# One Strassen level more in two places of a fused attention and MLP kernel, accumulator banks seeded by copies, and an instruction order that was searched

## The chip, the core and the metric

The kernel runs on one core of a Trainium2 chip. The metric is the device time of one execution in microseconds (us). A run gives several executions and I quote their median. An execution is marked slow when it is over 1.5% above the fastest of the same kernel. All other executions are marked fast; ratios use fast ones alone. The kernel before is run again beside every experiment on the same chip, and its median moved between 302.9 and 304.5 us, with single executions between 300.3 and 307.3. So differences under about 1% need the ratio to the kernel before with its interval.

The profile counts the work of four engines side by side: TensorE (PE; its weight loads are PEld), VectorE (DVE), ScalarE (ACT) and GpSimd (POOL), before the change busy for 94, 78, 59 and 34% of the span. The rows of a fifth, SyncE (SP), are here issues of transfers only.

## The reference, cut to what matters

```python
# q, k, v: (8 batches, 8 heads, 576 rows, 64); w_in: (512, 2048); w_out: (2048, 512)
def phi(x, c, s):                       # "features": 64 -> 128 columns
    r = np.maximum(x, 0.0)
    return np.concatenate([r * c, r * s], axis=-1)
kv  = einsum(phi(k), v);  z = sum(phi(k))
num = einsum(phi(q), kv); den = einsum(phi(q), z) + 1e-06
x = (num / den)                         # rearranged to (4608 tokens, 512)
h = x @ w_in                            # layer 1
g = h * np.cos(h)                       # "gate"
out = g @ w_out                         # layer 2, (4608, 512) fp32
```

A batch gives four tiles of 128 tokens and a rest of 64. The kernel forms nine groups of 512 tokens: 0 to 7, one per batch, and "r", which gathers the rests. The order of the groups is 0, 1, 2, 3, 4, 5, 6, r, 7.

## The kernel before

Every piece of work is an operation with a duration in us, an engine (or a choice of engines), what it depends on and which buffers it takes. A list scheduler walks through time and always gives the engine that is free first the ready operation of the best priority. The sequence that comes out is written, in that order, as the program of each engine.

```python
def run(self, cold=0.0):                        # class Plan, cut
    while ready:
        cand = []
        for o in ready:
            t = max([o.at] + [d.end + d.lat for d in o.deps])
            ...                                 # buffers free?
            for e, us in o.alts.items():
                cand.append((max(t, clock.get(e, 0.0)), e, us, o, t))
        t0, e0 = min((c[0], c[1]) for c in cand)
        t, _, us, o, _ = min((c for c in cand if c[1] == e0 and c[0] <= t0 + self.EPS),
                             key=lambda c: (..., c[3].prio, c[0]))
        ...
```

Layer 1 is plain: for each of 16 blocks of 128 rows of h, four matmuls of 512 columns, a sine on ACT (the cosine), a product on DVE (the gate).

```python
def moe1(key, g, js, cs, s0, s1):               # layer 1, TensorE
    for n, j in enumerate(js):
        for c in cs:
            nc.tensor.matmul(ps[key][:, n, :], lhsT=w_in_sb[:, c, j * P:(j + 1) * P],
                             rhs=x[:, c, s0:s1], start=(c == 0 and n == 0), ...)
def gate(key, dst):
    nc.vector.tensor_tensor(out=dst, in0=ps[key], in1=cosine, op=ALU.mult)
```

Layer 2 of groups 1 to 7 and r is one Strassen level: seven products of half the size instead of eight. It needs sums of the gates (1024 elements per partition each, SBUF to SBUF, all on DVE) and sums of finished products (five per group on DVE). Layer 2 of group 0 is plain.

```python
def sums(g, c, n):                              # sums of gates, always DVE
    out, in0, in1, op = ((s1, a21, a22, ALU.add), (s2, s1, a11, ALU.subtract),
                         (a21, a11, a21, ALU.subtract), (a12, a12, s2, ALU.subtract))[n]
    nc.vector.tensor_tensor(out=out, in0=in0, in1=in1, op=op)
...
e6 = op({"V": 0.69}, EV, lambda e: add(part(g, "u2"), g, "Y", "s1"), ...)   # 1 of 5 adds
```

## Time and profile before

| | before |
|---|---|
| device time, median (range) | 304.47 us (304.13 to 307.12) |
| span of the profiled execution | 298.7 us |
| matmuls; their issue time | 2565; 269.5 us |
| gaps on TensorE | 23.0 us, of it 1.2 at half clock |
| first matmul; last matmul to the end | 1.0 us; 5.0 us |

**Issue and gaps.** In the trace the starts of back-to-back matmuls lie 216 ns apart at 512 columns, 109 at 256, 56 at 128, about 30 at 65. The number of matmuls of each width times these is the issue time. What a distance between two starts has more than that is a gap. Where the gap falls in a stretch for which the trace records the half clock I count it, up to one interval per matmul, as half clock; the rest is a wait. I computed these sums from the matmul records.

The page's first two parts, before: busy us and share of the span, then the busy tenths of each engine in 40 slices of the span, and the TensorE clock in tenths.

```profile
PE 280.1 (94%) x2565; PEld 201.3 (67%) x2565; DVE 233.7 (78%) x450; ACT 175.6 (59%) x303; POOL 102.0 (34%) x107
...
PE   8879999899969987999979999999999999999993
...
DVE  1878888899995798887869798987786786768661
...
POOL 1370004396191686287077194011002001100500
PEclk9979999999999999999999999999999999999998
```

TensorE is the bottleneck. From 157 us on its row is all nines but for the last slice: after 200 us the gaps add up to 0.2 us.

What TensorE waited for, before (us in total, times, longest us):

```profile
engine line waited for: us in total, times, longest us
PE N L228 <- DVE x L241: 2.8, 2, 2.1
PE M L279 <- ACT xT L159: 2.6, 1, 2.6
PE PY L337 <- DVE s L309: 2.2, 2, 1.6
```

These are a numerator behind a ratio on DVE, layer 1 behind transposed x, and layer 2 behind a sum of gates.

The DVE sums of gates, before, by source line (count: shortest/median/longest ns, first and last start in us):

```profile
L309 DVE TENSOR_TENSOR s<-g x14: 680/681/1116, 71.6 to 283.0; 128x1024 f16<-128x1024 f16 x14
L309 DVE TENSOR_TENSOR s<-s,g x14: 679/681/1008, 73.4 to 283.8; 128x1024 f16<-128x1024 f16 x14
L309 DVE TENSOR_TENSOR g<-g x14: 676/682/684, 75.2 to 284.4; 128x1024 f16<-128x1024 f16 x14
L309 DVE TENSOR_TENSOR g<-g,s x14: 680/682/976, 81.3 to 287.8; 128x1024 f16<-128x1024 f16 x14
```

A sum takes 0.68 us. The longest reach 1.1 us, beside work on POOL.

Two stretches, before (start:end, length, then busy us of each engine, clock, DMA share, GB/s):

```profile
30.00:65.00 35.00, 33.68 (x330) 24.06 (x328) 30.32 (x69) 24.70 (x44) 11.68 (x16) 1.00 0.95 276
200.00:299.00 99.00, 93.94 (x679) 65.05 (x676) 67.52 (x105) 34.84 (x59) 10.45 (x20) 0.99 0.18 61
```

### The profile page before, as it was taken

To read this page: it belongs to the slowest core of one execution; us is meant where nothing else is said; L and a number is where in the kernel's file an instruction comes from. 1 tells how busy PE (TensorE), PEld (TensorE's weight loads), DVE (VectorE), ACT (ScalarE), POOL (GpSimd) and SP (SyncE) were. 2 spreads that over 40 slices of the span, in tenths; PEclk is the share of its full clock that TensorE was granted. 3 is DMA by queue.
4 is the path that set the end of the run, shared out by engine and by line. 5 is a ranking of instruction groups with operands and counts; after the bars stand their busy time and mean duration, and the time that the engine had idled before them with its cause. 6 is when DMAs were issued, how large, how long until landed. Compare 5 with 4: busy or idle time off the path is not lost.

```text
span 298.7 us, 6583 instructions
## 1 busy us (share of the span) xinstructions
PE 280.1 (94%) x2565; PEld 201.3 (67%) x2565; DVE 233.7 (78%) x450; ACT 175.6 (59%) x303; POOL 102.0 (34%) x107
## 2 busy tenths in 40 slices
PE   8879999899969987999979999999999999999993
PEld 8768856688855555566646666776666666566782
DVE  1878888899995798887869798987786786768661
ACT  2846748599379797679489497634433443443210
POOL 1370004396191686287077194011002001100500
PEclk9979999999999999999999999999999999999998
DMA  7799995897899999999999999715202100200213
GB/s 218 264 163 203 204 362 183 279 308 120 273 274 235 356 232 169 283 278 203 322 256 202 238 369 195 141 47 151 35 0 94 48 1 32 111 2 0 91 52 140
DMA packets 77086, 53.29 MB, mean 178 GB/s; under 512 B 46080, under 2 KB 74752, under 8 KB 77056
## 3 DMA queue, kind: packets, MB, share of 16 engines
q1 hardware_dynamic: 69760, 39.73, 55.2%
q0 software_dynamic: 6848, 12.59, 16.6%
q10 hardware_dynamic: 448, 0.57, 0.5%
q8 instruction: 20, 0.33, 0.5%
q14 instruction: 10, 0.08, 0.1%
HBM read 36.74 MB, written 9.44 MB: 155 GB/s over the span
## 4 chain that ended last, share of the span: by engine, by line
PE 55%; DMA 16%; DVE 10%; POOL 5%; SPq 5%; ACT 4%; issue 3%; ACTq 0%; DVEq 0%
PE M L279 26%; DMA vm<-in_v_dram 13%; PE PY L337 8%; PE PZ L337 6%; PE PX L337 5%; PE M L376 5%; POOL qp L181 4%; DMA qm<-in_q_dram 3%; PE KV L219 2%; DVE g L292 2%; SPq L171 2%; DVE x L241 2%; PE TP L263 2%; DVE s L309 2%; SPq L269 1%
## 5 line engine op out<-in xcount | busy, mean ns | idle before, releaser
L279 PE MATMUL M<-xT,w_in_sb 128*128 128x512 f16 (+1 forms) x640 | 120.2, 336 | 2.9 <-ACT xT L159 2.6
L286 ACT ACTIVATE ch<-M 128x512 f32<-128x512 f32 x144 | 84.9, 595 | 60.8 <-PE M L279 58.7
L292 DVE TENSOR_TENSOR g<-M,ch 128x512 f16<-128x512 f32 x128 | 85.8, 687 | 27.0 <-ACT ch L286 26.1
L279 PEld LDWEIGHTS <-w_in_sb 128*128 128x128 f16 x704 | 67.3, 98 | 46.6 <-issue 3.1
L181 POOL TENSOR_SCALAR qp<-qm,CS 128x512 f16<-128x512 f32 x29 | 60.0, 2074 | 31.0 <-DMA qm<-in_q_dram 27.0
L337 PEld LDWEIGHTS <-g 128*128 128x128 f16 x560 | 54.1, 98 | 11.5
L369 POOL DMA_DIRECT2D out_dram<-ost x14 | 7.8, 558 | 98.6 <-DVE ost L351 42.5
L179 ACT ACTIVATE kp<-km,CS 128x512 f16<-128x512 f32 x52 | 35.1, 715 | 0.2
L179 ACT ACTIVATE qp<-qm,CS 128x512 f16<-128x512 f32 x40 | 26.9, 713 | 11.9 <-DMA qm<-in_q_dram 11.9
L337 PE MATMUL PX<-w_out_sb,g 128*128 128x256 f16 x224 | 27.6, 273 | 0.0
L241 DVE TENSOR_TENSOR x<-N,rec 128x512 f16<-128x512 f32 (+1 forms) x44 | 26.1, 594 | 1.7 <-DVE rec L237 0.2
L337 PE MATMUL PY<-WT,g 128*128 128x256 f16 x224 | 27.2, 273 | 0.0
L337 PEld LDWEIGHTS <-s 128*128 128x128 f16 x224 | 21.4, 98 | 7.1 <-DVE s L309 2.8
L161 POOL CAST V<-vm 128x512 f16<-128x512 f32 (+1 forms) x22 | 13.9, 664 | 15.9 <-DMA vm<-in_v_dram 15.9
L228 PE MATMUL N<-kvz,qT 128*128 128x65 f16 x256 | 14.7, 196 | 2.3 <-DVE x L241 2.1
L228 PEld LDWEIGHTS <-qT 128*128 128x128 f16 x256 | 12.6, 100 | 6.1 <-issue 3.5
L337 PE MATMUL PY<-WT,s 128*128 128x256 f16 x112 | 14.1, 273 | 2.2 <-DVE s L309 2.2
L181 DVE TENSOR_SCALAR kp<-km,CS 128x512 f16<-128x512 f32 x28 | 15.5, 590 | 0.3 <-DMA km<-in_k_dram 0.2
L292 DVE TENSOR_TENSOR gr<-M,ch 128x512 f16<-128x512 f32 x16 | 10.9, 689 | 5.7 <-ACT ch L286 5.5
L219 PE MATMUL KV<-V,kp 128*128 128x65 f16 x320 | 12.9, 196 | 2.5 <-DVE kp L181 0.7
L279 PE MATMUL M<-xR,w_in_sb 128*128 128x512 f16 x64 | 15.1, 379 | 0.0
L219 PEld LDWEIGHTS <-kp 128*128 128x128 f16 x320 | 11.7, 99 | 4.7 <-issue 2.4
(70 smaller groups left out, 287.7 us busy)
## 6 DMA issues: line engine op xcount, KB each, us to landing
out_dram<-ost POOLq DMA_DIRECT2D x28, 256.0 KB, 4.1
qm<-in_q_dram SPq DMA_DIRECT2D x8, 640.0 KB, 5.3
km<-in_k_dram SPq DMA_DIRECT2D x8, 640.0 KB, 7.0
qm<-in_q_dram SPq DMA_DIRECT2D x8, 512.0 KB, 5.8
km<-in_k_dram SPq DMA_DIRECT2D x8, 512.0 KB, 8.8
vm<-in_v_dram SPq DMA_DIRECT2D x6, 640.0 KB, 8.1
vm<-in_v_dram SPq DMA_DIRECT2D x6, 512.0 KB, 8.9
w_in_sb<-in_moe_w_in_dram POOLq DMA_DIRECT2D x4, 512.0 KB, 9.0
```

The costliest lines, as they stand in the source:

```text
L161: (nc.vector if eng == "V" else nc.gpsimd).tensor_copy(out=out, in_=in_)
L179: nc.scalar.activation(out=dst, in_=src, func=AF.Relu, scale=sc)
L181: (nc.vector if eng == "V" else nc.gpsimd).tensor_scalar(out=dst, in0=src, scalar1=0.0, scalar2=sc, op0=ALU.max, op1=ALU.mult)
L219: nc.tensor.matmul(tile_[:, n, hh, :], lhsT=kps[b][:, t, h].rearrange("p g d -> p (g d)"), rhs=V1[:, t, h, :], start=(t == 0), stop=(t == NT))
L228: nc.tensor.matmul(tile_[:, n, hh, :], lhsT=qT(p, t)[:, h, :], rhs=kvzs[p][:, h, :], start=(i == 0), stop=(i == len(parts) - 1))
L241: nc.vector.tensor_tensor(out=dst, in0=tile_[:, :, :, 0:D], in1=rec.unsqueeze(3).broadcast_to((P, nb, HB, D)), op=ALU.mult)
L279: nc.tensor.matmul(ps[key][:, n, :], lhsT=w_in_sb[:, c, j * P:(j + 1) * P], rhs=x[:, c, s0:s1], start=(c == 0 and n == 0), stop=(c == NCT ...
L286: nc.scalar.activation(out=ps[("ch", key)], in_=ps[key].rearrange("p j s -> p (j s)"), func=AF.Sin, bias=math.pi / 2.0, scale=1.0)
L292: nc.vector.tensor_tensor(out=dst, in0=m, in1=ps[("ch", key)].rearrange("p (j s) -> p j s", s=m.shape[2]), op=ALU.mult)
L337: nc.tensor.matmul(ps[(g, bank)][:, i, :], lhsT=lhs[:, j, i * P:(i + 1) * P], rhs=rhs[:, j], start=(first and i == 0 and j == 0), stop=(j ...
L369: e0.dma_start(out=five[:, t0:t0 + 2, :], in_=blocks(ost, n))
L376: nc.tensor.matmul(ps[("M2", t)], lhsT=gts[0][:, j, t * P:(t + 1) * P], rhs=w_out_sb[:, j, :], start=(j == 0), stop=(j == NJT - 1))
```

## The change

It saves matmul time by two more Strassen levels: in layer 1 of groups 6, r and 7, and in layer 2 of group 0. To pay for their sums it seeds an accumulator bank with a copy of another product, so that TensorE adds; it lets POOL take sums; and it takes the instruction order from a search, whose model had a lock: of the DVE and POOL operations marked "p" it ran only one at a time.

```diff
-    def run(self, cold=0.0):
-        ... list scheduler ...
+    def run(self):
+        return [(self.ops[int(x.rstrip("VAG"))], x.lstrip("0123456789"))
+                for x in ORDER.split()]
+ORDER = """
+25 180 24 115 229 22 184 883 342 818 230 21 40V 42V 41A 44V 43A 60 45V 46A 62 61V 64 47A 63V 35A
+... 75 lines more: an operation's number, and V, A or G for DVE, ACT or POOL ...
+"""
@@ layer 1 of groups 6, r, 7: seven products of a quad of blocks, three banks @@
+        bank, first, lhs, rhs = (
+            ("X", True, a11, x_block(g, 0, 0)), ("Z", True, ws[0], xs[0]),
+            ("Y", False, ws[1], xs[1]), ("X", False, a12, x_block(g, 1, 0)),
+            ("Y", False, s3, x_block(g, 0, 1)), ("Z", False, ws[2], x_block(g, 1, 1)),
+            ("Y", False, a22, xs[2]))[n]
+            p1 = mm(0, xs + ys[-1:], [X], rx)
+            p5 = mm(1, [xsum[0], wsum1[0], p1] + ..., [Z], [slot])
+            y1 = op({"A": 0.6, "V": 0.69}, EV, y_seed, deps=[p1, p5], ...)   # copy X to bank Y
+            e5 = op({"A": 0.6, "V": 0.69}, EV, evac5, deps=[p5, ga], acq=[q5])
+            p6 = mm(2, [xsum[1], wsum1[1], y1], [], [slot])                  # adds onto the copy
+            z1 = op({"V": 0.69}, EV, z_add, deps=[p6, e5])
+            p7 = mm(4, [xsum[2], s3_done(), z1], [], rx)
+            c = op({"V": 0.69}, EV, c22, deps=[p7])
+            ... p2, p3, p4 and the four gates ...
@@ sums may go to POOL: "p" marks what the model's lock keeps apart @@
-                st[(c, n)] = op({"V": 0.69}, (1, i, c, n), lambda e, c=c, n=n: sums(g, c, n), ...)
+    WSUM = {"Vp": 1.24, "Gp": 4.1}
+    XSUM = {"Vp": 0.42, "Gp": 1.2}
+    SUM0 = {"Vp": 0.7, "Gp": 2.15}
+                st[(c, n)] = op(SUM0, (1, i, c, n), lambda e, c=c, n=n: sums(e, g, c, n), ...)
@@ features on POOL have no "p" @@
+                    {"A": 0.71, "Vp": 0.5} if cut else {"A": 0.71, "Vp": 0.5, "G": 2.1},
@@ layer 2: group 0 too; its copies may be ACT or DVE; also: q tiles one by one, last product split @@
-    layer2_plain(lambda t, n: (1, 1, t, n))
+    layer2(0, lambda i: (1, 1, i))
```

The first of the eight pieces of the weights to be loaded were, before, the four of w_in and then the four of w_out.

## The prediction

> **What bounds it now.** TensorE. The page's busy table gives PE 280.1 us of a 298.7 us span (94%), DVE 78%, ACT 59%, POOL 34%. In the timeline matmul starts are 216 ns apart at 512 columns, 109 at 256, 56 at 128, about 30 at 65; times the counts of the groups table, 269.8 us of matmul issue. The other 29 us: 1.0 before the first matmul, 23.0 of gaps, 5.0 from the last matmul to the end. The gaps: 9.3 us before 30 us (first inputs), then stalls of about 2.4 at 50-60, 3.1 at 80-90 (layer 1 waits for transposed x), 3.5 at 100-120 (layer 2 waits for DVE sums), 2.6 at 150-160 (a numerator waits for a DVE ratio queued behind other work). From 180 to 294 us they sum to 0.6 us.
>
> **The change, costed.**
> - Layer 1 Strassen in three groups: 3x64 matmuls of 216 ns (41.4 us) become 3x112 of 109 ns (36.6): -4.8 us, in the region without gaps, so all counts.
> - Group 0's layer 2 becomes Strassen: 13.8 to 12.2 us, -1.6. Two cover matmuls: +0.4. Issue falls to about 263.9 us.
> - Seeding a bank by a copy cuts layer 2's adds that must be DVE from 5 to 2 per group; the rest are copies for ACT (0.60) or DVE (0.68). Each layer 1 quad adds two copies and two adds. Many 1024-element sums go from DVE to POOL; some features go from ACT to DVE. I estimate from counts and durations DVE about 243 us, ACT 178, POOL over 150: DVE 84%, still under PE.
> - [...] a 1024-element sum takes 0.68 us alone, up to 1.12 beside POOL work; the DVE feature 0.48, up to 0.90; a gate reading PSUM stays at 0.69. More POOL work means more collisions, unless the order avoids them.
> - q tiles become one per token tile (four buffers) instead of one of five, freeing the feature-transpose-load chain that the chain of waits shows at 58-90 us.
> - The last product is split and its rows stored singly: last matmul to end, 5.0 to about 4.3 us.
>
> **On the critical path.** -5.9 issue, -0.6 tail, and half of the 13.7 us of gaps after 30 us: -6.5. New: +0.5 in the Strassen chains. Startup stays.
>
> **Prediction: 292 us**, 8 in 10 within 286 to 298.5. Faster by over 2%: 0.88; within 2%: 0.11; slower: 0.01.
>
> **What would show it.** Matmul issue near 264 us at unchanged intervals; gaps after 30 us of 5-9 us, those at 80-90 and 100-120 gone; the last 100 us under 3 us of gaps; POOL busy 150 us or more; the last matmul about 4 us before the end.
>
> **What would make it wrong.** (1) Long POOL sums lengthen DVE, and layer 1's seeded chain (product, copy, product, add, product) stalls PE in the last 100 us. (2) The middle is supplied by DMA (nine tenths busy from 40 to 185 us), and the early saving only becomes waiting. (3) The searched order assumes durations the chip doesn't keep, so engines wait in new places. Or better: stalls almost vanish, near 286.

The sum: 304.5 - 5.9 - 0.6 - 6.5 + 0.5 = 292.

## The result, and the profile after

| | before | after |
|---|---|---|
| device time, median (range) | 304.47 us (304.13 to 307.12) | 317.03 us (315.9 to 317.53) |
| ratio | | 1.0388, 95% interval 1.0323 to 1.0452: slower |
| span of the profiled execution | 298.7 | 314.1 |
| matmuls; issue time | 2565; 269.5 | 2759; 263.9 |
| gaps; of it half clock | 23.0; 1.2 | 44.2; 6.1 |
| last matmul to the end | 5.0 | 5.2 |

A ratio here is the mean time of one kernel's fast runs over that of the other's of the same rounds, so it is not quite the ratio of the medians.

The account closes: issue -5.6, gaps +21.2, tail +0.2, together +15.8 for spans that differ by 15.4. The saving of issue came nearly as predicted (5.6 us of 5.9). The gaps, which were to shrink, nearly doubled.

The same two parts of the page, after:

```profile
PE 281.8 (90%) x2759; PEld 221.5 (70%) x2759; DVE 258.6 (82%) x455; ACT 182.1 (58%) x332; POOL 195.4 (62%) x154
...
PE   8787876799798999999789997999999999898992
...
DVE  1874699989699899988968979999888789988861
...
POOL 1350065949759439987904889478976796484540
PEclk9977999799999999999979999999999999999999
```

POOL's busy time doubled. TensorE has sevens and eights in the first half, and the clock row has sevens at 16 to 31, 55 to 63 and 157 to 165 us. They are half-clock stretches of 3.4 us from 15.7, 26.0, 56.7 and 159.1 us; apart from the end of the span, the kernel before has only one, from 16.4 us. The last three began near waits of TensorE of 2.0, 2.3 and 2.8 us, which ended at 26.1, 55.5 and 158.0 us.

What TensorE waited for, after:

```profile
engine line waited for: us in total, times, longest us
PE KV L253 <- ACT kp L215: 3.1, 3, 1.4
PE N L262 <- DVE x L282: 2.9, 2, 1.8
PE SD L436 <- DVE s L338: 2.8, 1, 2.8
PE KV L253 <- DVE kp L217: 2.3, 1, 2.3
PE M L325 <- DMA w_in_sb<-in_moe_w_in_dram: 2.0, 1, 2.0
PE M L325 <- DVE g L338: 1.9, 2, 1.6
PE YZ L381 <- DVE p L338: 1.5, 1, 1.5
```

Sums of gates (s), ratios (x) and features (kp) on DVE, a piece of w_in, and in the last line the new layer 1 chain.

The DVE sums of gates, after:

```profile
L338 DVE TENSOR_TENSOR g<-M,ch x110: 675/682/693, 24.4 to 293.0; 128x512 f16<-128x512 f32 x110
...
L338 DVE TENSOR_TENSOR s<-s,g x12: 676/692/4562, 51.1 to 299.5; 128x1024 f16<-128x1024 f16 x12
L338 DVE TENSOR_TENSOR s<-g x9: 681/687/4111, 50.1 to 298.8; 128x1024 f16<-128x1024 f16 x9
L338 DVE TENSOR_TENSOR g<-g,s x9: 678/681/3920, 58.8 to 303.4; 128x1024 f16<-128x1024 f16 x9
L338 DVE TENSOR_TENSOR g<-g x8: 673/778/2605, 53.4 to 298.2; 128x1024 f16<-128x1024 f16 x8
```

The medians are still 0.68 us, but the longest are 2.6 to 4.6 us. The gates, which read the matmul's result from PSUM, keep to 0.68 us to the last one. Here is the longest, on DVE:

```profile
189.55 4.56 DVE L338 TENSOR_TENSOR s<-s,g 128x1024 f16<-128x1024 f16 x1
194.04 0.68 DVE L338 TENSOR_TENSOR g<-M,ch 128x512 f16<-128x512 f32 x1
```

and at the same time on POOL:

```profile
189.35 2.14 POOL L338 TENSOR_TENSOR g<-g 128x1024 f16<-128x1024 f16 x1
191.43 2.12 POOL L338 TENSOR_TENSOR g<-g,s 128x1024 f16<-128x1024 f16 x1
193.54 2.44 POOL L217 TENSOR_SCALAR qp<-qm,CS 128x512 f16<-128x512 f32 x1
```

The DVE sum came 0.2 us after POOL's first sum and got through only when both of POOL's sums were done. TensorE then waited 2.0 us for a ratio queued behind it. Another, of 4.11 us, came on DVE at 153.1 us, 0.5 us into a POOL feature of 2.0 us, and got through only after that feature and the 2.1 us POOL sum behind it. The kernel's plan has the lock, but it has it between operations marked "p": the planned DVE sum starts when the lock is free. In the trace DVE's sums start while POOL's operations run. Only beside POOL's two-input sums did DVE's take so long: no 1024-element sum that ran beside POOL's features or copies alone took over 1.14 us.

I laid all 1608 operations of the plan beside the trace. In my replay of the plan, whose durations and dependences are written in the kernel, TensorE ends at about 285 us; the chip follows it within 0.2 us to about 16 us, is 8.9 us late at 63, 13 at 158, 17.5 at 196 and 23.7 at the end. ACT's and POOL's operations last as planned (together 3.2 us more). DVE's operations with SBUF operands alone last about 27 us longer than planned; its others do not.

A second thing happened early. The transfer queue, and POOL just then, after:

```profile
23.32 0.60 SPq L207 DMA_DIRECT2D qm<-in_q_dram  x1
23.96 0.63 SPq L209 DMA_DIRECT2D qm<-in_q_dram  x1
42.63 0.60 SPq L207 DMA_DIRECT2D km<-in_k_dram  x1
```

```profile
39.52 2.50 POOL L338 TENSOR_TENSOR s<-g 128x1024 f16<-128x1024 f16 x1 [16.23 <-DVE g L338]
41.97 0.64 POOL L562 CAST km<-w_out_sb 2x1 f32<-2x1 f16 x1
```

The loads of k for batch 1 wait for the tiny copy on POOL, which stands in order behind a sum, which waits 16 us for gates. The plan doesn't contain the copies. Before, this load was issued at 35.3 us, after at 42.6. The q loads, on the other hand, went out at 23.3 us, beside the weights.

The two stretches after:

```profile
30.00:65.00 35.00, 26.99 (x279) 22.86 (x277) 30.53 (x49) 21.61 (x36) 16.59 (x14) 0.95 0.72 181
200.00:314.00 114.00, 105.37 (x975) 88.53 (x972) 91.96 (x145) 55.67 (x102) 70.12 (x54) 0.99 0.27 70
```

From 30 to 65 us TensorE was busy 27.0 us against 33.7, and the transfers ran at 0.72 of their share against 0.95.

### The profile page after: what moved, and what is told of

It is laid out like the page before. It is cut to its first block, busy times and chain, and to the rows that moved or that the text cites. A ratio compares the mean times of both kernels' runs of the same rounds, so it can differ in the third digit from the quotient of the medians.

```text
span 314.1 us, 7073 instructions
## 1 busy us (share of the span) xinstructions
PE 281.8 (90%) x2759; PEld 221.5 (70%) x2759; DVE 258.6 (82%) x455; ACT 182.1 (58%) x332; POOL 195.4 (62%) x154
## 5 line engine op out<-in xcount | busy, mean ns | idle before, releaser
L325 PE MATMUL M<-xT,w_in_sb 128*128 128x256 f16 (+1 forms) x512 | 94.1, 334 | 5.4 <-DMA w_in_sb<-in_moe_w_in_dram 2.0
L387 ACT ACTIVATE ch<-M 128x512 f32<-128x512 f32 x116 | 67.6, 596 | 46.6 <-PE M L325 32.3
L338 DVE TENSOR_TENSOR g<-M,ch 128x512 f16<-128x512 f32 x110 | 72.9, 685 | 17.9 <-ACT ch L387 17.6
L436 PEld LDWEIGHTS <-g 128*128 128x128 f16 x640 | 61.9, 98 | 16.3 <-issue 2.3
L217 POOL TENSOR_SCALAR qp<-qm,CS 128x512 f16<-128x512 f32 x16 | 33.3, 2081 | 10.9 <-DMA qm<-in_q_dram 9.8
L338 POOL TENSOR_TENSOR s<-g 128x1024 f16<-128x1024 f16 x7 | 15.2, 2178 | 30.9 <-DVE g L338 30.3
L217 POOL TENSOR_SCALAR kp<-km,CS 128x512 f16<-128x512 f32 x13 | 27.2, 2094 | 2.7 <-DMA km<-in_k_dram 2.6
L215 ACT ACTIVATE kp<-km,CS 128x512 f16<-128x512 f32 x30 | 20.2, 714 | 1.6 <-DMA km<-in_k_dram 1.6
L217 DVE TENSOR_SCALAR kp<-km,CS 128x512 f16<-128x512 f32 x37 | 20.7, 585 | 0.4 <-DMA km<-in_k_dram 0.4
L338 POOL TENSOR_TENSOR g<-g 128x1024 f16<-128x1024 f16 x8 | 18.0, 2256 | 3.0 <-DVE s L338 2.8
L436 PE MATMUL PZ<-w_out_sb,g 128*128 128x256 f16 x128 | 16.6, 273 | 1.4 <-DVE g L338 1.4
```

Source lines behind the costliest of these rows:

```text
L215: nc.scalar.activation(out=dst, in_=src, func=AF.Relu, scale=sc)
L217: (nc.vector if eng == "V" else nc.gpsimd).tensor_scalar(out=dst, in0=src, scalar1=0.0, scalar2=sc, op0=ALU.max, op1=ALU.mult)
L338: (nc.vector if eng == "V" else nc.gpsimd).tensor_tensor(out=out, in0=in0, in1=in1, op=op)
L387: nc.scalar.activation(out=ps[("ch", key)], in_=ps[key].rearrange("p j s -> p (j s)"), func=AF.Sin, bias=math.pi / 2.0, scale=1.0)
L436: nc.tensor.matmul(ps[(g, bank)][:, i, :], lhsT=lhs[:, j, i * P:(i + 1) * P], rhs=rhs[:, c * HJ // 2 + j], start=(first and i == 0 and j = ...
```

## The experiments

Eighteen kernels ran, all with correct results. The quoted expectations name theories: M, the order was made for durations that the chip does not keep; D, the work that Strassen adds cannot be hidden; G0, this holds for group 0, whose Strassen product falls where the kernel is tightest; P, S and L are explained where e1 is expected. Times are medians; "ratio" is to the kernel before of the same rounds, from fast executions alone. In the tables, "wait+half" are waits and half clock.

### Sums off POOL, and the weights and first loads

e1: the 46 two-input operations that the order gives to POOL go to DVE, at the same places of the order.

```diff
-... 143V 181G 177 ... 175V 182G 243 ... 301V 196G 302V ... 397 884G 876 ...
+... 143V 181V 177 ... 175V 182V 243 ... 301V 196V 302V ... 397 884V 876 ...
```

> Edit: every two-input operation that the order gives to POOL (46 of them: sums of g, x sums, weight sums, some gates) goes to DVE at the same place in the order; nothing else changes. Theory P [...]: the changed kernel's DVE was held about 27 us beyond its planned durations by POOL work (single 1024-element sums of 2.6 to 4.6 us against 0.69), and the PE waits of 3.0 us at 155, 2.0 us at 194 and 1.7 us at 266 follow from that; without POOL sums no DVE sum should take over 1.2 us, those three waits go, and the time falls by 8 to 13 us, to 304-309. Theory S (supply: the first loads after the start leave late, all else follows): at most 3 us less than 317. Theory L (layer 1 Strassen chains are too long): no gain or a loss, since DVE gets 46 more operations (about +31 us of work).

e2: sums stay on POOL; the weights are loaded in their natural order, and the loads of k and v of batch 1 are issued right after those of q.

```diff
-... 71 15G 59A ... 55A 7G 77V ... 73 11G 87V ... 167V 236 200 ... 192V 238 202 ...
+... 71 7G 59A ... 55A 11G 77V ... 73 13G 87V ... 233 236 238 241 243 246 248 99A ...
```

> Edit: the eight weight loads go out in their natural order (four of layer 1 first), and the six k and v loads of batch 1 come right after its two q loads in the order, so that the small POOL copies that hold them no longer stand behind a POOL sum that waits for gates until 39.5 us. Theory S: by 63 us the changed kernel is 8.9 us behind the plan that its order comes from; the loads go out at about 34-35 us as in the kernel before, the PE waits for weights at 24-26 us (2 us and a half-clock window) and at 41-62 us shrink, and the time falls by 5 to 9 us, to 308-312. Theory P alone: at most 2 us less.

e3: both edits.

> Edit: e1 and e2 together. If P and S are separate costs that add: 14 to 20 us less than the changed kernel, 297-303, so under the kernel before (304.5). If they are one cost (whatever is late is late once): about the larger of the two alone, 305-309. Theory L expects over 306 in any case, with PE gaps of 5 us or more after 200 us.

| | time | ratio (95%) | issue | wait+half | of it 30-65 us | of it after 200 us | DVE busy |
|---|---|---|---|---|---|---|---|
| before (profile) | 304.47 | 1 | 269.5 | 21.8+1.2 | 2.6+0 | 0.2+0 | 233.7 |
| after (profile) | 317.03 | 1.0388 (1.0323-1.0452) | 263.9 | 38.1+6.1 | 9.4+1.6 | 6.5+0 | 258.6 |
| e1 | 308.92 | 1.0210 (1.0138-1.0282) | 263.6 | 31.9+4.3 | 8.4+3.1 | 7.1+0 | 262.4 |
| e2 | 316.47 | 1.0440 (1.0351-1.0529) | 263.8 | 39.5+6.2 | 10.9+2.1 | 6.7+0 | 258.3 |
| e3 | 304.40 | 1.0068 (0.9997-1.0138) | 263.8 | 30.7+1.6 | 7.0+1.6 | 7.2+0 | 262.6 |

The same sums, on DVE alone, in the groups of instructions of e1 (after the count: busy us in total, mean ns of one, then idle us before them):

```profile
L338 DVE TENSOR_TENSOR s<-s,g 128x1024 f16<-128x1024 f16 x16 | 11.3, 709 | 0.2
L338 DVE TENSOR_TENSOR s<-g 128x1024 f16<-128x1024 f16 x16 | 11.0, 688 | 0.2
```

Giving DVE 46 operations more made its busy time longer by only 3.8 us and the kernel faster: from e2 to e3, in the same rounds, the sums are worth 12.1 us; from after to e1, in other rounds, 8.1 by the medians and 5 by the ratios. Of DVE's 258.6 us after the change, then, a good part was not work: in e1, with no sum on POOL, the groups of DVE's 1024-element sums of gates average 0.69 to 0.73 us, where after the change single ones took up to 4.56. The edit takes away two things at once, the collisions and sums that POOL does slowly (2.1 us against 0.68); no run parts them. The weights and loads alone (e2) gain nothing, because DVE is then what batch 1 waits for (TensorE waited 4.1 us for kp and 3.1 for a denominator); with the sums off POOL (e1 to e3) they are worth 4.5 us. e1 shows why: freed from POOL's sum, all loads of batch 1 went out from 23.8 us on, beside the weights, and the last piece of w_out landed at 46.0 us, where it lands at 38.9 in e3; TensorE waited 5.2 us for w_out.

e1 met theory P's forecast (no 1024-element sum on DVE took over 1.11 us), e2 missed theory S's. e3 fell between its own two, and shows the waits after 200 us that theory L expected. The two edits together make up for the whole loss. They don't give the gain: e3 has 5.7 us less issue than before and 9.3 us more gaps.

e4: the order itself in question. After's operations, no sums on POOL, but put in order by before's list scheduler.

```diff
-        return [(self.ops[int(x.rstrip("VAG"))], ...) for x in ORDER.split()]
+        ... before's list scheduler ...
```

> Edit: the changed kernel's operations, but ordered by the kernel before's list scheduler (earliest start, then priority, no lock) in place of the written order, with two-input sums allowed on DVE alone. Issue stays 264 us. If only the written order is at fault (P or S), the Strassen layer 1 and the seeding pay even in a plain order: 296-302. Theory L: over 304, with gaps after 200 us.

325.63 us, ratio 1.0762. Of its 48.2 us of waits 19.5 lie after 200 us. The list scheduler handles the plain layer 1 without a gap there, and handles the new chains badly. So the searched order is not bad as such: for the new chains it is far better than the old method.

### Parts of the change undone within the same order

e5: layer 2 of group 0 plain again, on e3.

```diff
+    for t in T:                                 # new operations, numbered after the others
+        for h in range(2):
+            op({"PE": 1.73}, (0,), lambda t=t, h=h: plain2(t, range(8 * h, 8 * h + 8)))
+    for t in T:
+        op({"A": 0.6, "V": 0.69}, (0,), lambda e, t=t: plain2_out(e, t))
 ... in ORDER they stand in place of the Strassen operations of group 0, which are left out ...
```

> Edit: e3 (no POOL sums, early loads), and group 0's layer 2 done plainly again (64 matmuls of 512 columns, no sums, no seeds; the eight weight-sum operations after it). Issue rises by 1.6 us to 265.5. In e3 the stretch from 20 to 65 us still loses 11.7 us in waits and a half-clock window, against 4.1 us before the change. Theory G0 (Strassen in group 0's layer 2 has nothing to hide its copies and sums behind): 4 to 7 us of that go, so e5 is 3 to 6 us under e3 (304.4), at 298-302. Rival (the early loss is the written order's and the DMA's): e5 within 1.5 us of e3 or slower.

314.44 us, ratio 1.0378. This test was flawed by my placement: the eight sums of w_out (0.69 us each) stood on DVE in front of batch 1's k features, and TensorE waited 8.3 us for kp. It says nothing about theory G0.

e6: layer 1 of groups 6, r, 7 plain again, on e3.

```diff
-            p1 .. p7, seeds, adds (Strassen quads)
+    for g in (6, "r", 7):
+        for j in range(NJT):
+            op({"PE": 0.87}, ..., moe1(("M1", g, j), g, [j], range(NCT), 0, SM))
```

> Edit: e3 with layer 1 of the last three groups plain again at the places of the Strassen products (16 units of 4 matmuls a group; x sums, weight sums, seed copies and adds of layer 1 dropped). Issue rises by 4.8 us to 268.6. In e3 DVE is busy 95% from 200 to 280 us (73% before the change) and PE waits 7.2 us after 200 us (0.2 before). Theory D (layer 1 Strassen spends in DVE work what it saves on PE): the waits after 200 us fall to about 1-2 us and the time stays within 2 us of e3. If layer 1 Strassen is a plain gain, e6 is 4 us or more over e3. If it is a plain loss, e6 is 3 us or more under e3.

306.40 us, ratio 1.0119 (1.0033 to 1.0206) against 1.0068 of e3. Issue rose by 4.6 us, and the time by 2.0 by the medians, with intervals that overlap: here the Strassen level of layer 1 seems to give back more than half. But the waits after 200 us, for which theory D forecast 1 to 2 us, stayed at 5.5 in this order.

e7: the copies into banks and out of them that the order gives to DVE go to ACT, on e3. The kernels differ in 22 operations, not in the 24 of the expectation. e8: e7 with e5's plain group 0.

```diff
-... 469 967V 472 ...
+... 469 967A 472 ...
```

> Edit: e3 with every bank copy that the order gives to DVE (seeds, fifth products, finished banks: 24 of them at 0.69 us) on ACT (0.60 us) at the same place. After 200 us ACT is busy 52%, DVE 95%. Theory D: DVE falls to about 80% there, the waits after 200 us shrink from 7.2 to 2-4 us, and the time falls by 3 to 5 us, to 299-301. Rival (the chain product, copy, product, add is what PE waits for, not DVE's load): less than 1.5 us of change.

> Edit: e5 and e7 together. If both theories hold and the costs add, 294-298, more than 2% under the kernel before. If either falls, 299-304.

e7: 303.27 us, ratio 1.0006 (0.9917 to 1.0094), waits after 200 us 5.0 instead of 7.2. From 200 to 280 us DVE's busy share fell from 95% in e3 to 90%, not to 80%, and ACT's rose from 53% to 61%. The time fell by 1.1 us by the medians: that is the rival's forecast and not theory D's 3 to 5, though the intervals of the ratios overlap. So 2.2 of the 7.2 us of waits went with the copies, and 5.0 stayed. e8: 311.7 us, with e5's flaw; both of its forecasts were missed.

### New orders for all, half and none of the Strassen parts

The remaining question was whether e3's gaps belong to the order or to the operations. I searched orders anew by random moves on a replay of the operations with the durations measured in these traces (a DVE feature, for one, took 0.48 us alone and before the change up to 0.90 beside POOL's work), with no two-input sum on POOL, for as long for each of four kernels: all of the change, layer 1 plain, group 0 plain, both plain.

```diff
-ORDER = """ 25 180 24 115 229 22 184 883 342 818 230 21 40V 42V 41A 44V 43A 60 45V ...
+ORDER = """ 40A 54G 180 25 21 230 24 22 115 42A 44V 43V 4G 5G 9G 56G 7G 13G 15G ...   (e9)
```

> All operations of the change with both Strassen parts, in an order searched anew, with no two-input sum on POOL: the search replayed the operations with the durations measured in the traces of the runs so far (DVE features lengthened beside POOL features, the POOL copies ahead of the first loads, transfer times and landings as traced). That replay, which put the earlier runs within 3 us of what they measured, gives 288. Theory M (the loss is the order, made for durations that the chip does not keep): 286 to 294, ratio about 0.95 to 0.97, gaps of TensorE below 22 us with issue still 263.9. Theory D (the added work for DVE cannot be hidden, whatever the order): not below 300.

> As e9, but layer 1 of the last three groups plain; the order searched for as long, in the same way. The replay gives 289. If the Strassen level in layer 1 is worth its 4.6 us of issue once the order is right, this is 3 to 5 us slower than e9; if its chains give the issue back as waits, within 2 us of it.

> As e9, but layer 2 of group 0 plain as before the change, Strassen kept in layer 1 of the last three groups; order searched for as long. The replay gives 284. Theory G0 (the early Strassen product puts eight weight sums, six sums of gates and two accumulator sums on DVE at 30 to 55 us, where DVE is what batch 1 waits for, and costs more than its 1.6 us): 2 to 5 us faster than e9. If the early Strassen level is a gain: 1 to 2 us slower than e9.

> As e9, but both Strassen parts undone, with the other changes (copies as seeds in layer 2, q tiles one by one, no cover lost) kept; order searched for as long. Issue 270. The replay gives 289. It tells how much of e11 is owed to the searched order alone: against e11 it should be 3 to 5 us slower if layer 1 Strassen is worth its issue; against the kernel before, 10 to 16 us faster if the order alone removes the gaps of 30 to 165 us.

| | Strassen in layer 1 / group 0 | time | ratio (95%) | issue | wait+half | 30-65 us | 100-150 us | after 200 us |
|---|---|---|---|---|---|---|---|---|
| e9 | yes / yes | 311.77 | 1.0271 (1.0222-1.0320) | 263.8 | 34.8+7.1 | 8.4+1.5 | 6.9+3.3 | 8.1+0 |
| e10 | no / yes | 310.46 | 1.0187 (1.0125-1.0249) | 268.6 | 27.2+4.3 | 6.8+1.5 | 5.7+1.6 | 1.3+0 |
| e11 | yes / no | 310.42 | 1.0218 (1.0161-1.0275) | 265.2 | 32.8+3.0 | 2.7+0 | 6.8+1.6 | 7.5+0 |
| e12 | no / no | 309.36 | 1.0187 (1.0128-1.0246) | 270.1 | 26.1+4.1 | 3.4+0 | 8.7+1.3 | 0.5+0 |

My replay said 284 to 289, and the chip 309 to 312: I had repeated the mistake that I was studying. A search finds the orders that look best in its model, so it leans on whatever the model has wrong; the same replay was within 3 us for orders that had not been searched against it. Part of what it had wrong lay at 100 to 150 us, where all four stood 7 to 10 us. Since e12, with neither Strassen part, is no better than the others (e10's four fast executions have a median of 309.3), these four do not decide between theories M and D. The transfer queue there, in e11:

```profile
120.95 7.84 SPq L314 DMA_TRANSPOSE qT<-qp  x2
128.89 0.61 SPq L206 DMA_DIRECT2D vm<-in_v_dram  x1
```

A transpose often takes 1.2 to 1.3 us to issue (in the trace after, 1.24 us at 84.7 us and 1.20 at 116.7); these two took 7.8 together. What held them is not shown. What came behind in the queue was issued later too (128.9). My replay let them all be issued at once, and let a store of an output tile take no share.

e13 to e15 were searched with transfers issued as late as in these traces, the stores in between, half-clock stretches, and transfers 15% slower as a second case. They shared one more defect: pieces of the weights swapped and the first loads beside them again. e16 to e18 have the weights in before's order.

> All operations of the change, sums on DVE only, order searched against the replay corrected by the traces of e9 to e12 [...], at the traced transfer times and at 15% longer ones. The replay gives 288 and 303 for the two; its optimism on orders searched against it was 5 to 20 us before. Theory M: under 300. Theory D: 300 or more, and slower than the run with both parts undone.

> As e13 with layer 2 of group 0 plain (Strassen in layer 1 of the last three groups kept). The replay gives 284 and 289, which is the least sensitive to slow transfers of the three. If the early Strassen product is what cannot be hidden (G0): under 297 and at least 4 us under e13.

> As e13 with both Strassen parts undone. The replay gives 288 and 290. If layer 1 Strassen is a gain in an order made for it, this is 3 to 5 us slower than e14; if its chains give the issue back, within 2 us of e14; waits after 200 us below 1.5 us here, against 3 to 8 us with Strassen in layer 1.

> All operations of the change, sums on DVE only, weights in the order of before and the first loads of batch 1 after them. The replay gives 288; it was 20 us too low for e13. Theory M: under 300. Theory G0 (the Strassen product of group 0 cannot be hidden): 303 to 310, waits at 30 to 65 us again 5 us or more.

> As e16 with layer 2 of group 0 plain. The replay gives 283; it was 17 to 20 us too low for e14, of which some 6 us came from the late weights. So 296 to 300, ratio to before 0.975 to 0.99; no half-clock window at 40 to 48 us; waits after 200 us still 4 to 6 us.

> As e16 with both Strassen parts undone. The replay gives 293 (the search found less here). It was 15 us too low for e15, of which some 6 us came from the late weights: 300 to 303. If layer 1 Strassen is a gain in a sound order, e17 is 3 to 5 us faster than this; if its chains give it back, the two are within 2 us.

| | Strassen in layer 1 / group 0 | time | ratio (95%) | issue | wait+half | 30-65 us | 100-150 us | after 200 us |
|---|---|---|---|---|---|---|---|---|
| e13 | yes / yes | 310.40 | 1.0243 (1.0194-1.0291) | 263.8 | 35.8+2.8 | 8.0+0 | 1.0+0 | 10.0+1.5 |
| e14 | yes / no | 303.89 | 1.0029 (0.9986-1.0072) | 265.3 | 26.9+3.9 | 5.8+2.7 | 2.6+0 | 5.9+0 |
| e15 | no / no | 303.91 | 1.0040 (0.9997-1.0082) | 270.0 | 20.7+4.3 | 7.2+2.4 | 0.6+0 | 0.4+0 |
| e16 | yes / yes | 305.00 | 1.0055 (1.0005-1.0106) | 263.8 | 29.2+3.0 | 7.4+0 | 0.9+0 | 8.7+1.6 |
| e17 | yes / no | 302.95 | 0.9970 (0.9924-1.0017) | 265.3 | 24.0+4.9 | 5.2+2.3 | 1.8+0 | 5.3+0 |
| e18 | no / no | 309.62 | 1.0086 (0.9994-1.0178) | 270.0 | 25.8+4.5 | 7.0+2.8 | 1.7+0 | 0.6+0 |

The corrections, all made at once, helped where they were made: the stretch from 100 to 150 us fell from 7 to 10 us of gaps to 0.6 to 2.6. But e17, the best, only equals the kernel before, and my expectations for it (296 to 300) and for e14 (under 297) were missed; the half clock that I expected gone from e17 at 40 to 48 us came at 44 to 51. e13, over 300 and slower than e15, fits theory D, and e16 (305.0, 7.4 us of waits at 30 to 65) fits G0, but e17 and e18 stand as long there. e15 is within 2 us of e14, as expected if the level in layer 1 gives its issue back. e18's median rests on runs from 304.3 to 311.0, and only two of the six, 304.3 and 308.2, are marked fast, so I lean on its trace more than on its time.

What TensorE waited for after 200 us in e17, with Strassen in layer 1:

```profile
PE PZ L435 <- DVE PZ L337: 1.6, 1, 1.6
PE YZ L380 <- DVE p L337: 0.8, 1, 0.8
PE YZ L380 <- DVE g L337: 0.7, 1, 0.7
```

The same view of e15 and of e18, both plain, is empty. This stretch is the clearest result of the series. There the transfers are mostly over (their share is 0.18 before and 0.27 after):

- Strassen in layer 1, thirteen kernels of two ways of searching and some edited by hand (e4 left out): 5.0 to 11.5 us of gaps after 200 us.
- Plain layer 1 in an order made for it (before, e10, e12, e15, e18): 0.2 to 1.3 us. Only e6, the plain form squeezed into the other's order, has 5.5.

The four pairs that were searched alike and whose operations differ in this level alone give its price by stretch: e9 against e10 6.8 us more waits after 200 us, e11 against e12 7.0, e14 against e15 5.5, e17 against e18 4.7. The level saves 4.6 to 4.9 us of issue. So in this stretch it costs as much as it saves, or more. The times of the pairs, each with an order of its own, don't agree: by the ratios the Strassen kernel is 0.8% slower in e9 against e10, within 0.4% in the next two pairs, and 1.2% faster in e17 against e18. That last difference is what e18's expectation calls a gain, but it rests on e18's two fast runs, and e18's trace loses it elsewhere: after 200 us the pair is even. The likely reason is in the code of the change: product, copy, product, add, product, add, product. Each step goes from TensorE to DVE or ACT and back, on engines that are busy with gates, and only a few banks are there to work on something else meanwhile. That it is this chain, and not DVE's load, is argued and not shown: from 200 to 280 us DVE is 89 to 90% busy in e7 and e17 and 74% in e15, and no run keeps the chain and frees DVE.

For group 0 the four pairs that differ in it alone (each with an order of its own) agree less than their medians suggest. By the ratios the kernel with Strassen is 0.5% slower in e9 against e11 and 0.9% in e16 against e17, with intervals that overlap, 2.1% slower in e13 against e14, and equal in e10 against e12. The issue is 1.4 to 1.5 us less, so none of them gains. But theory G0, that batch 1 suffers at 30 to 65 us, is not shown: there Strassen costs 7.2 us in e9 against e11 and 4.9 in e10 against e12, but nothing in the other two pairs (8.0 against 8.5 and 7.4 against 7.5). e13 and e16 lose their time after 200 us instead (11.5 against 5.9 and 10.3 against 5.3), far from group 0's product, so that there the order found is as likely the cause. e15 and e18, with neither part, also stand 9.6 and 9.8 us at 30 to 65 us, against 2.6 before.

## Why the prediction was wrong, point by point

- **Bound by TensorE; issue 263.9 us; intervals unchanged.** Right: 263.9 us, the same intervals.
- **DVE about 243 us, POOL over 150, ACT 178.** 258.6, 195 and 182. The direction was right; DVE's figure had no lengthening beside POOL's sums in it, and its operations with SBUF operands alone lasted about 27 us longer than planned.
- **"a 1024-element sum takes 0.68 us alone, up to 1.12 beside POOL work … More POOL work means more collisions, unless the order avoids them."** The direction was right, and the trust in "unless" was wrong. I took 1.12 us, the longest case before, for the size of a collision; after, they last up to 4.56.
- **The step that failed: "half of the 13.7 us of gaps after 30 us: -6.5. New: +0.5 in the Strassen chains."** In its place the gaps after 30 us went from 13.7 to 31.6 us, 3.3 of them half clock, and those before 30 us from 9.3 to 12.5. Two causes are shown by edits. POOL's two-input sums: 5 to 12 us (after to e1; e2 to e3). The order of the weights and first loads, made for a plan without the copies that gate them: 4.5 us (e1 to e3). A third goes with the new Strassen products of layer 1: after 200 us the gaps rose by 6.3 us, where I had allowed 0.5, and stayed at 5 us and more in every order tried; that their chains, not DVE's load, make these gaps is argued.
- **"those at 80-90 and 100-120 gone."** Half right: at 100 to 120 us 3.6 us fell to 0.5, at 80 to 90 us 3.1 only to 2.8. From 65 to 100 us they rose from 3.3 to 4.9.
- **"the last matmul about 4 us before the end."** Wrong by a little: 5.2 us, as before (5.0). The forecast 0.7 us of the split last product doesn't show.
- **"What would make it wrong (3): the searched order assumes durations the chip doesn't keep."** and **(1)**: both came true. (2), a middle that the transfers supply too slowly, was not tested by itself; from 30 to 65 us their share fell from 0.95 to 0.72. I gave "slower" 0.01, as if one could write down such a risk and still trust the order.

Open remains how much a better order could do. None of the nine orders of all the change's operations beat the kernel before, nor did the ten kernels with parts undone; e17 comes out at 0.997 with an interval that holds 1. That no order can is not shown. The change's other parts (copies as seeds in layer 2, q tiles one by one, the split last product) are in all of these kernels; no run undoes them, so what they cost or save is not known.

## What to carry to other kernels

A saving of issue time on the bottleneck is a saving only if the chain that feeds it doesn't get longer: count the trips to other engines that a cheaper algorithm adds per product, and compare that stretch's gaps before and after. An order found by search is tuned to its model's faults as much as to the chip, so put every instruction into the model (also the tiny copies), take its durations, and how long an issue of a transfer takes, from traces of orders like the one that it proposes, and expect the chip to give back the surplus. Before giving sums to the idle GpSimd, look whether DVE has SBUF-only operations at that time (after the change such a sum took up to 4.56 us beside POOL's sums, a gate read from PSUM at most 0.69): moving 46 two-input operations back to the busier engine made this kernel faster (316.47 to 304.40 us, e2 to e3).
